# Attention products with v on half-width column tiles, two heads at a time

## Chip, cores and metric

The kernel runs on one core of a Trainium2 chip. The metric is the device time of one execution in microseconds. TensorE is written PE below (PEld for its weight loads), VectorE DVE, ScalarE ACT, GpSimd POOL, SyncE SP.

## What is computed

Causal attention with a learned decay (4 batches, 8 heads, 576 positions, 64 columns a head), then two feed-forward blocks (2304 tokens, 512 -> 2048 -> 512):

```python
cum = np.cumsum(np.log(np.clip(f, 0.0001, 1.0)), axis=-1)
scores = np.matmul(q, k.transpose(0, 1, 3, 2)) / np.sqrt(D) + cum[:, :, :, None] - cum[:, :, None, :]
attn = softmax(np.where(causal, -1e9, scores))
x = np.matmul(attn, v)                        # 2304 x 512
x = (s * np.maximum(x @ w_in, 0) ** 2 + b) @ w_out
x = leaky_relu(x @ w2_in, 0.01) @ w2_out
```

Nearly every operand of a product is kept as a sum of two parts, a rounded one and its rest, so that a product of two such operands is made of three or four products.

## The kernel before

**Units.** Attention is cut into units of one batch: its queries 0 to 255 (`first`) or 256 to 575 (`rest`). Unit 0 has a path of its own (`first_a` to `first_c`). Units 1 to 3 are `first` units, 4 to 7 `rest` units. A unit has 8 heads, taken as 4 pairs. A `first` pair gives two tiles, one per head, each with both query blocks of 128. A `rest` pair gives five: query block 3 for each head, block 2 for each head, and one **half** tile, in which the last 64 queries of both heads stand side by side.

**Stages of a tile.** `st_score` makes the scores on PE (line 296: two heads on different halves of the array's rows), adds the decay and finds the maximum on DVE (line 327), and exponentiates on ACT (line 345). `st_split` divides by the sum and stores p as two float16 parts: line 370 on ACT the rounded one, line 371 on DVE the rest, into `p_hl` (three buffers). A DMA transpose issued from SP then writes `p_t` (three buffers). `st_av` multiplies: for each block of 128 keys and each part of p, line 393 loads as weights both parts of v, 64 columns each, side by side on the array's 128 columns, and streams the transposed p. PSUM tile `ps_v` so holds two halves, p times the rounded v in one half of the partitions and p times the rest in the other. Line 412 copies one half to `x_raw` on ACT, line 413 adds the other on DVE. When both heads of a pair are there, lines 427 and 428 split x into two float32r parts for the first feed-forward block, and for the half tile line 423 scales x on POOL and a DMA stores it for the last unit.

**What sets the order.** `slots_to` issues the stages of tile i, i-1 and i-2 (`LAG` is 2) between the 16 blocks of the first feed-forward layer of an earlier unit (`mlp1_h` line 705, `mlp1_o` lines 746 and 749, with g made in lines 727 to 730). Inside that a list scheduler places each instruction by priority; `run_on` ties the products of one `st_av` call to each other, from the second one on. Each engine then works strictly in the order written. The second layer (lines 807 and 823) comes when all attention is done.

Of the kernel before, what the change touches and what calls it, by code (L numbers as in the profile page):

```python
# [8 lines left out]
F32 = mybir.dt.float32  # L9
F32R = mybir.dt.float32r  # L10
F16 = mybir.dt.float16
# [3 lines left out]
ALU = mybir.AluOpType  # L15
AX = mybir.AxisListType

P = 128
UN = 256
# [19 lines left out]
def attention_moe_moe_kernel(  # L39
# [15 lines left out]
    nc = tc.nc  # L55
    B, H, D, S = vT.shape
# [10 lines left out]
    NL = S - 2 * UN  # L67
# [125 lines left out]

    qk_p, cumk, v_raw, v_st, v_inv = {}, {}, {}, {}, {}
    s_t, t_t, p_hl, p_t, av_t, sm_t = {}, {}, {}, {}, {}, {}
    xs, x_raw = {}, {}

    def load_pair(p):
        if p >= NP:
# [66 lines left out]
    def run_on(first):  # L266
        return nullcontext() if first else tc.high_priority(offset=P_RUN)
# [82 lines left out]
    def last_of_pair(jb):  # L350
        u, h, j, half = jobs[jb]
        return half or (h % 2 == 1 and units[u][2] == UN)

    def st_split(i):

        jb, n, ts, last = tiles[i]
        nt = len(ts)
        tt, sm = t_t.pop(i), sm_t.pop(i)
        nc.vector.tensor_scalar(sm[:, 4 : 4 + nt], sm[:, 2 : 2 + nt], 1.0e-9, 1.0 / PSCALE, ALU.add, ALU.mult)
        nc.vector.reciprocal(sm[:, 6 : 6 + nt], sm[:, 4 : 4 + nt])  # L360
        ph = ap.tile([P, 10 * P], F16, tag="p_hl", name="p_hl", bufs=3)
        at = to = 0
        for r, t in enumerate(ts):
            w = sum(QT[t])
            nk = -(-w // P)
            e, inv = tt[:, at : at + w], sm[:, 6 + r : 7 + r]
            v = ph[:, to : to + 2 * nk * P].rearrange("p (l c) -> p l c", l=2)
            if nk * P > w:
                nc.gpsimd.memset(v[:, :, w:], 0.0)
            nc.scalar.mul(v[:, 0, :w], e, inv)  # L370
            nc.vector.scalar_tensor_tensor(v[:, 1, :w], e, inv, v[:, 0, :w], ALU.mult, ALU.subtract)  # L371
            at += w
            to += 2 * nk * P
        p_t[i] = pt = ap.tile([P, 10, P], F16, tag="p_t", name="p_t", bufs=3)
        nc.sync.dma_start_transpose(out=pt[:, : to // P], in_=ph[:, :to])

    def st_av(i):
        jb, n, ts, last = tiles[i]
        u, h, j, half = jobs[jb]
        b, u0, un, _ = units[u]  # L380
        if half or (n == 0 and h % 2 == 0):
            av_t[j // 2] = ps_a.tile([P, 512], F32, tag="ps_v", name="ps_v", bufs=2)
        av, pt = av_t[j // 2], p_t.pop(i)
        to = 0
        for t in ts:
            q0, m = QT[t]
            nk = -(-(q0 + m) // P)
            at = 0 if half else q0 - u0 + h % 2 * UN
            for e in range(P // m):
                for k in range(nk):  # L390
                    for l in range(2):
                        with run_on(t == ts[0] and e == k == l == 0):
                            nc.tensor.matmul(  # L393
                                av[:, at + e * m : at + (e + 1) * m],
                                v_st[j + e][:, k].rearrange("p l d -> p (l d)"),
                                pt[:, to + l * nk + k, e * m : (e + 1) * m],
                                start=(k == 0 and l == 0),
                                stop=(k == nk - 1 and l == 1),
                            )
            to += 2 * nk  # L400
        if not last:
            return
        pr = h // 2
        if not half and h % 2 == 0:
            x_raw[u] = xp.tile([P, UN + NL], F32, tag="x_raw", name="x_raw", bufs=2)
        xr = x_raw[u]
        at = UN if half else 0
        for e in range(2) if half else [h % 2]:
            own, oth = slice(e * D, (e + 1) * D), slice((1 - e) * D, (2 - e) * D)
            m = NL if half else UN  # L410
            src, o = av[:, e * m : (e + 1) * m], xr[own, at : at + m]
            nc.scalar.copy(o, src[oth])
            nc.vector.tensor_tensor(out=o, in0=src[own], in1=o, op=ALU.add)
        if not last_of_pair(jb):
            return
        if pr == 0:
            xs[u] = xp.tile([P, 2, ND, UN], F32R, tag="x", name="x", bufs=2)
        inv = v_inv[j - j % 2][:, 4:5]
        with ahead(P_X):
            split_x1(xs[u], pr, xr[:, :UN], inv)  # L420
            if un > UN:
                xl = xr[:, UN:]
                nc.gpsimd.tensor_scalar(xl, xl, inv, 0.0, ALU.mult, ALU.add)
                nc.sync.dma_start(out=xld[pr * P : (pr + 1) * P, b * NL : (b + 1) * NL], in_=xl)

    def split_x1(x, d, raw, inv):
        nc.scalar.mul(x[:, 0, d], raw, inv)
        nc.vector.scalar_tensor_tensor(x[:, 1, d], raw, inv, x[:, 0, d].bitcast(F32), ALU.mult, ALU.subtract)
# [151 lines left out]
    def first_b(h):  # L580
# [4 lines left out]
        at = 0  # L585
# [2 lines left out]
            nc.gpsimd.tensor_scalar(e[:, at : at + w], e[:, at : at + w], r[:, t : t + 1], 1.0, ALU.mult, ALU.mult)  # L588
            at += w
        ps = ps_a.tile([P, 512], F32, tag="ps_v", name="ps_t0", bufs=2)  # L590
        pt = pt_0[h] = ap.tile([P, 5 * P], F32, tag="p_t", name="pt_0", bufs=3)

        to = 0
        for k in range(NT0):
# [369 lines left out]
```

## Time and profile before

| | us |
|---|---|
| median of 3 runs | 1044.53 |
| lowest, highest | 1044.37, 1044.60 |
| the profiled execution | 1039.49 |
| its span, first to last instruction | 1037.7 |
| PE busy | 986.1 |
| DVE busy | 537.9 |
| ACT busy | 521.3 |
| products with v (line 393), PE busy | 59.7 |

The profile is that of one execution, which took 5.0 us less than the median. "Busy" counts the time in which an engine has at least one instruction in work; the matmuls of PE overlap, so what one costs is read from start to start on the timeline. The rows on which the prediction rests stand below.

### The profile page before, as it was taken

To read this page: it belongs to the slowest core of one execution; us is meant where nothing else is said; L and a number is where in the kernel's file an instruction comes from. 1 tells how busy PE (TensorE), PEld (TensorE's weight loads), DVE (VectorE), ACT (ScalarE), POOL (GpSimd) and SP (SyncE) were. 2 spreads that over 40 slices of the span, in tenths; PEclk is the share of its full clock that TensorE was granted. 3 is DMA by queue.
4 is the path that set the end of the run, shared out by engine and by line. 5 is a ranking of instruction groups with operands and counts; after the bars stand their busy time and mean duration, and the time that the engine had idled before them with its cause. 6 is when DMAs were issued, how large, how long until landed. Compare 5 with 4: busy or idle time off the path is not lost.

```text
span 1037.7 us, 18127 instructions
## 1 busy us (share of the span) xinstructions
PE 986.1 (95%) x6664; PEld 851.0 (82%) x6664; DVE 537.9 (52%) x1410; ACT 521.3 (50%) x1283; POOL 151.8 (15%) x234
## 2 busy tenths in 40 slices
PE   7887789989999999999999999999999999999998
PEld 4676679879888888888999998778888888888897
DVE  6899773665667766777531399873111311211111
ACT  4777696655656766677643566552221221221232
POOL 4434424110101010100000135430000000000000
PEclk9899999999999999999999999999999999999999
DMA  8499491566889999989620463701000100100010
GB/s 282 152 245 269 89 211 40 136 134 134 186 155 181 180 179 197 185 170 192 90 83 2 168 239 94 239 13 49 33 1 1 61 1 1 41 0 1 1 41 21
DMA packets 184296, 116.68 MB, mean 112 GB/s; under 512 B 137040, under 2 KB 163152, under 8 KB 184208
## 3 DMA queue, kind: packets, MB, share of 16 engines
q1 hardware_dynamic: 184208, 115.53, 47.0%
q8 instruction: 52, 0.85, 0.3%
q14 instruction: 36, 0.29, 0.1%
HBM read 74.00 MB, written 10.04 MB: 81 GB/s over the span
## 4 chain that ended last, share of the span: by engine, by line
PE 47%; issue 3%; DVE 3%; POOL 2%; DMA 1%; ACT 1%; POOLq 0%; SPq 0%; ACTq 0%; DVEq 0%
PE ps_o L823 17%; PE ps_h L807 16%; PE ps_o L749 6%; PE ps_h L705 6%; POOL w L111 2%; PE ps_v L393 1%; DVE wt L103 1%; DMA w_raw<-in_moe_w_out 1%; DVE wt L105 1%; DVE wt L102 1%; PE ps_s L296 1%; DMA p_t<-p_hl 0%; ACT wt L101 0%; PE ps_s L283 0%; DVE g L730 0%
## 5 line engine op out<-in xcount | busy, mean ns | idle before, releaser
L705 PE MATMUL ps_h<-x,w 128*128 128x256 f32 x1728 | 242.9, 286 | 5.0 <-POOL w L111 3.3
L749 PE MATMUL ps_o<-g,w 128*128 128x256 f32 (+1 forms) x1536 | 226.8, 289 | 10.8 <-ACT g L729 6.3
L705 PEld LDWEIGHTS ps_h<-x,w 128*128 128x128 f32 x1728 | 220.4, 190 | 7.7 <-POOL w L111 3.9
L823 PE MATMUL ps_o<-w,g 128*128 128x512 f32 x864 | 216.1, 396 | 1.8 <-DVE g L815 1.8
L807 PE MATMUL ps_h<-x,w 128*128 128x512 f32 (+1 forms) x960 | 213.6, 370 | 0.0
L749 PEld LDWEIGHTS ps_o<-g,w 128*128 128x128 f32 x1536 | 197.3, 190 | 17.5 <-ACT g L729 7.9
L807 PEld LDWEIGHTS ps_h<-x,w 128*128 128x128 f32 x960 | 169.0, 188 | 34.4
L823 PEld LDWEIGHTS ps_o<-w,g 128*128 128x128 f32 x864 | 160.5, 188 | 41.5 <-DVE g L815 3.5
L815 DVE TENSOR_TENSOR g<-ps_h,g 128x512 fp32r<-128x512 f32 (+1 forms) x80 | 51.0, 637 | 258.3 <-ACT g L814 258.1
L813 ACT ACTIVATE ps_h<-ps_h 128x512 f32<-128x512 f32 (+1 forms) x80 | 43.1, 539 | 250.7 <-PE ps_h L807 250.7
L345 ACT ACTIVATE tt<-tt,sm 128x512 f32<-128x512 f32 (+4 forms) x128 | 76.0, 594 | 46.5 <-DVE sm L327 45.2
L371 DVE SCALAR_TENSOR_TENSOR p_hl<-tt,sm,p_hl 128x512 f16<-128x512 f32 (+4 forms) x128 | 77.5, 619 | 34.3 <-ACT p_hl L370 33.8
L370 ACT ACTIVATE p_hl<-tt,sm 128x512 f16<-128x512 f32 (+4 forms) x128 | 73.2, 595 | 40.2 <-DMA p_t<-p_hl 31.6
L111 POOL TENSOR_TENSOR w<-wt,w 128x512 fp32r<-128x512 f32 x48 | 73.6, 1537 | 98.0 <-ACT w L110 92.2
L730 DVE TENSOR_TENSOR g<-ps_h,g 128x256 fp32r<-128x256 f32 x128 | 53.6, 421 | 60.9 <-ACT g L729 59.6
L393 PE MATMUL ps_v<-p_t,v_st 128*128 128x128 f16 (+1 forms) x912 | 59.7, 211 | 14.7 <-DMA p_t<-p_hl 11.9
L727 ACT ACTIVATE ps_h<-ps_h 128x256 f32<-128x256 f32 x128 | 46.8, 367 | 50.3 <-PE ps_h L705 49.4
L393 PEld LDWEIGHTS <-v_st 128*128 128x128 f16 x912 | 44.3, 98 | 21.4 <-issue 13.2
L327 DVE CUSTOM_DVE_ANT_0 tt<-ps_s,cumk 128x512 f32<-128x512 f32 (+4 forms) x128 | 59.6, 497 | 2.2 <-PE ps_s L287 0.7
L101 ACT ACTIVATE wt<-w_raw 128x512 f32<-128x512 f32 x64 | 42.7, 672 | 28.2 <-POOL w L111 19.8
L729 ACT CAST g<-ps_h 128x256 fp32r<-128x256 f32 x128 | 47.2, 370 | 7.9 <-PE ps_o L749 4.4
L728 ACT ACTIVATE ps_h<-ps_h 128x256 f32<-128x256 f32 x128 | 46.9, 368 | 3.0
(91 smaller groups left out, 859.9 us busy)
## 6 DMA issues: line engine op xcount, KB each, us to landing
w_raw<-in_moe_w_in SPq DMA_DIRECT2D x32, 512.0 KB, 5.3
w_raw<-in_moe_w_out SPq DMA_DIRECT2D x32, 512.0 KB, 5.8
cumk<-cumd SPq DMA_DIRECT2D x32, 256.0 KB, 3.9
qk_p<-in_qk SPq DMA_DIRECT2D x16, 480.0 KB, 4.8
x1d<-x1o SPq DMA_DIRECT2D x36, 128.0 KB, 2.9
cumk<-cumd SPq DMA_DIRECT2D x32, 144.0 KB, 3.1
v_raw<-in_v SPq DMA_DIRECT2D x16, 288.0 KB, 3.3
out<-o SPq DMA_DIRECT2D x18, 256.0 KB, 2.3
```

Of the source, the lines that this page charges most:

```text
L111: nc.gpsimd.tensor_tensor(w[:, 1], x, w[:, 0].bitcast(F32), ALU.subtract)
L327: nc.vector.tensor_tensor_reduce(tt[:, at + k0 : at + k0 + kw], ps[:, c, :kw] if half else ps[:, h % 2, at : at + w], cumk[jb][:, k0 : k0 ...
L345: nc.scalar.activation(e, e, AF.Exp, bias=sm[:, r : r + 1], scale=-1.0, accum_out=sm[:, 2 + r : 3 + r])
L370: nc.scalar.mul(v[:, 0, :w], e, inv)
L371: nc.vector.scalar_tensor_tensor(v[:, 1, :w], e, inv, v[:, 0, :w], ALU.mult, ALU.subtract)
L393: nc.tensor.matmul(av[:, at + e * m : at + (e + 1) * m], v_st[j + e][:, k].rearrange("p l d -> p (l d)"), pt[:, to + l * nk + k, e * m : ( ...
L705: nc.tensor.matmul(ps, wi[:, a, d * P : (d + 1) * P], x[:, c, d], start=(d == 0 and n == 0), stop=(d == ND - 1 and n == 2),)
L730: nc.vector.tensor_tensor(out=g[:, 1, :UN], in0=ps, in1=g[:, 0, :UN].bitcast(F32), op=ALU.subtract)
L749: nc.tensor.matmul(po[d], wo[:, a, d * P : (d + 1) * P], g[:, c], start=(first and n == 0), stop=(last and n == 2),)
L807: nc.tensor.matmul(ps[:, :n], wi[:, a, d * P : (d + 1) * P], x[:, e, d, :n], start=(d == 0 and k == 0), stop=(d == ND - 1 and k == 2),)
L815: nc.vector.tensor_tensor(out=g[:, 1, :n], in0=raw, in1=g[:, 0, :n].bitcast(F32), op=ALU.subtract)
L823: nc.tensor.matmul(po[m], g[:, a, m * P : (m + 1) * P], wo[:, e, :], start=(i == 0 and k == 0), stop=(i == NF - 1 and k == 2),)
```

## The change

`st_av` returns at once for the first head of a pair and works at the second head for both. For each block of 128 keys it makes four products per head (each part of v with each part of p), each with 64 columns of weights: head 0 on columns 0 to 63 of the array and partitions 0 to 63 of PSUM, head 1 on columns 64 to 127 and partitions 64 to 127. The four accumulate in PSUM, so that the tile holds x for both heads, and the half tile's queries lie behind the other 256 in the same `ps_v` tile. `x_raw` with its copies and sums is gone, `split_x1` reads PSUM, and the half tile is scaled on ACT. The transposed p has five buffers.

```diff
@@ -193,7 +193,7 @@
 
     qk_p, cumk, v_raw, v_st, v_inv = {}, {}, {}, {}, {}
     s_t, t_t, p_hl, p_t, av_t, sm_t = {}, {}, {}, {}, {}, {}
-    xs, x_raw = {}, {}
+    xs = {}
 
     def load_pair(p):
         if p >= NP:
@@ -371,56 +371,50 @@
             nc.vector.scalar_tensor_tensor(v[:, 1, :w], e, inv, v[:, 0, :w], ALU.mult, ALU.subtract)
             at += w
             to += 2 * nk * P
-        p_t[i] = pt = ap.tile([P, 10, P], F16, tag="p_t", name="p_t", bufs=3)
+        p_t[i] = pt = ap.tile([P, 10, P], F16, tag="p_t", name="p_t", bufs=5)
         nc.sync.dma_start_transpose(out=pt[:, : to // P], in_=ph[:, :to])
 
     def st_av(i):
         jb, n, ts, last = tiles[i]
         u, h, j, half = jobs[jb]
         b, u0, un, _ = units[u]
-        if half or (n == 0 and h % 2 == 0):
-            av_t[j // 2] = ps_a.tile([P, 512], F32, tag="ps_v", name="ps_v", bufs=2)
-        av, pt = av_t[j // 2], p_t.pop(i)
-        to = 0
+        if not half and h % 2 == 0:
+            return
+        j -= j % 2
+        if not half and n == 0:
+            av_t[j] = ps_a.tile([P, 512], F32, tag="ps_v", name="ps_v", bufs=2)
+        av = av_t[j]
+        pts = [p_t.pop(i)] if half else [p_t.pop(i - 1), p_t.pop(i)]
+        to, first = 0, True
         for t in ts:
             q0, m = QT[t]
             nk = -(-(q0 + m) // P)
-            at = 0 if half else q0 - u0 + h % 2 * UN
-            for e in range(P // m):
-                for k in range(nk):
-                    for l in range(2):
-                        with run_on(t == ts[0] and e == k == l == 0):
+            at = q0 - u0
+            for k in range(nk):
+                for lv, lp in ((0, 0), (0, 1), (1, 0), (1, 1)):
+                    for e in range(2):
+                        q = pts[0][:, to + lp * nk + k, e * m : (e + 1) * m] if half else pts[e][:, to + lp * nk + k]
+                        with run_on(first):
                             nc.tensor.matmul(
-                                av[:, at + e * m : at + (e + 1) * m],
-                                v_st[j + e][:, k].rearrange("p l d -> p (l d)"),
-                                pt[:, to + l * nk + k, e * m : (e + 1) * m],
-                                start=(k == 0 and l == 0),
-                                stop=(k == nk - 1 and l == 1),
+                                av[e * D : (e + 1) * D, at : at + m],
+                                v_st[j + e][:, k, lv],
+                                q,
+                                start=(k == lv == lp == 0),
+                                stop=(k == nk - 1 and lv == lp == 1),
                             )
+                        first = False
             to += 2 * nk
-        if not last:
+        if not last_of_pair(jb):
             return
         pr = h // 2
-        if not half and h % 2 == 0:
-            x_raw[u] = xp.tile([P, UN + NL], F32, tag="x_raw", name="x_raw", bufs=2)
-        xr = x_raw[u]
-        at = UN if half else 0
-        for e in range(2) if half else [h % 2]:
-            own, oth = slice(e * D, (e + 1) * D), slice((1 - e) * D, (2 - e) * D)
-            m = NL if half else UN
-            src, o = av[:, e * m : (e + 1) * m], xr[own, at : at + m]
-            nc.scalar.copy(o, src[oth])
-            nc.vector.tensor_tensor(out=o, in0=src[own], in1=o, op=ALU.add)
-        if not last_of_pair(jb):
-            return
         if pr == 0:
             xs[u] = xp.tile([P, 2, ND, UN], F32R, tag="x", name="x", bufs=2)
-        inv = v_inv[j - j % 2][:, 4:5]
+        inv = v_inv[j][:, 4:5]
         with ahead(P_X):
-            split_x1(xs[u], pr, xr[:, :UN], inv)
+            split_x1(xs[u], pr, av[:, :UN], inv)
             if un > UN:
-                xl = xr[:, UN:]
-                nc.gpsimd.tensor_scalar(xl, xl, inv, 0.0, ALU.mult, ALU.add)
+                xl = xp.tile([P, NL], F32, tag="x_l", name="x_l", bufs=2)
+                nc.scalar.mul(xl, av[:, UN:un], inv)
                 nc.sync.dma_start(out=xld[pr * P : (pr + 1) * P, b * NL : (b + 1) * NL], in_=xl)
 
     def split_x1(x, d, raw, inv):
@@ -588,7 +582,7 @@
             nc.gpsimd.tensor_scalar(e[:, at : at + w], e[:, at : at + w], r[:, t : t + 1], 1.0, ALU.mult, ALU.mult)
             at += w
         ps = ps_a.tile([P, 512], F32, tag="ps_v", name="ps_t0", bufs=2)
-        pt = pt_0[h] = ap.tile([P, 5 * P], F32, tag="p_t", name="pt_0", bufs=3)
+        pt = pt_0[h] = ap.tile([P, 5 * P], F32, tag="p_t", name="pt_0", bufs=5)
 
         to = 0
         for k in range(NT0):
```

The built program holds 1824 products on 64 columns in place of 912 on 128. Counted over PE's whole order, the form of the array (128 rows by 128 columns, 64 by 128, 128 by 64) changes 256 times, before 119 times.

PE in a `rest` unit before, where the block of products of the second head begins (v_st_5879 is that head's v, p_t_6103 its transposed p, ps_v_6105 the pair's PSUM tile):

```order
L307 LDWEIGHTS ident_h_74
L307 MATMUL ps_s_6266<-mask_h_75,ident_h_74 128x128
L749 MATMUL ps_o_5437<-g_5744,w_1443 128x256 x6
L393 LDWEIGHTS v_st_5879
L393 MATMUL ps_v_6105<-p_t_6103,v_st_5879 128x128
```

The eight products of one head run between those of the feed-forward layer; the first head's block stands in another place.

PE in a `rest` unit now, the same place (v_st_5716 and v_st_5718 are the pair's two heads):

```order
L743 MATMUL ps_o_4570<-g_5551,w_1902 128x256 x6
L699 MATMUL ps_h_5732<-x_4648,w_161 128x256 x2
L398 LDWEIGHTS v_st_5716
L398 MATMUL ps_v_6000<-p_t_5893,v_st_5716 64x128
L398 LDWEIGHTS v_st_5718
L398 MATMUL ps_v_6000<-p_t_5980,v_st_5718 64x128
```

The two heads alternate, each with its own load, for 32 products; the tile of 256 queries and the half tile follow as runs of 24 and 40.

ACT before, at the end of a `rest` pair (lines 727 to 729 make g, 763 ends a unit):

```order
L412 COPY x_raw<-ps_v 64x256
L728 ACTIVATE ps_h<-ps_h 128x256
L729 CAST g<-ps_h 128x256
L427 ACTIVATE x<-x_raw,vs 128x256
L412 COPY x_raw<-ps_v 64x64
L763 ACTIVATE x1o<-ps_o,sb 128x256
L345 ACTIVATE tt,sm<-tt,sm 128x576
```

ACT now, at the end of such a pair (lines 721 to 723 make g):

```order
L723 CAST g<-ps_h 128x256
L421 ACTIVATE x<-ps_v,vs 128x256
L345 ACTIVATE tt,sm<-tt,sm 128x576
L417 ACTIVATE x_l<-ps_v,vs 128x64
L370 ACTIVATE p_hl<-tt,sm 128x576
```

The copies are gone, and a scaling of 64 columns has come, behind the split.

## Rows read from the trace of the kernel before

**Rows 1.** The page, span and busy time of each engine.

```profile
span 1037.7 us, 18127 instructions
...
PE 986.1 (95%) x6664; PEld 851.0 (82%) x6664; DVE 537.9 (52%) x1410; ACT 521.3 (50%) x1283; POOL 151.8 (15%) x234
```

**Rows 2.** Stretches: length, busy PE, PEld, DVE, ACT, POOL (instructions), clock, DMA share, GB/s.

```profile
40.00:160.00 120.00, 100.38 (x720) 88.09 (x719) 102.40 (x326) 90.21 (x261) 44.34 (x37) 0.95 0.77 188
160.00:520.00 360.00, 345.28 (x3110) 307.97 (x3109) 236.44 (x735) 237.95 (x613) 39.94 (x97) 1.00 0.79 155
520.00:600.00 80.00, 80.00 (x672) 79.90 (x672) 26.89 (x61) 36.79 (x97) 6.02 (x35) 1.00 0.27 94
```

**Rows 3.** Groups by shape: products with v, what reads them, their split.

```profile
L393 PE MATMUL ps_v<-p_t,v_st 128*128 128x128 f16 x592 | 47.8, 221 | 14.1 <-DMA p_t<-p_hl 11.2 <-DMA v_st<-v_hl 2.8
...
L413 DVE TENSOR_TENSOR x_raw<-ps_v,x_raw 64x256 f32<-64x256 f32 x56 | 23.5, 419 | 7.9 <-ACT x_raw L412 7.0
...
L412 ACT COPY x_raw<-ps_v 64x256 f32<-64x256 f32 x56 | 20.6, 367 | 1.7 <-PE ps_v L393 0.3
...
L427 ACT ACTIVATE x<-x_raw,vs 128x256 fp32r<-128x256 f32 x28 | 14.0, 502 | 6.1 <-DVE x_raw L413 4.3 <-PE ps_h L705 1.5
...
L393 PE MATMUL ps_v<-p_t,v_st 128*128 128x64 f16 x320 | 12.1, 193 | 0.6 <-DMA p_t<-p_hl 0.6
...
L763 ACT ACTIVATE x1o<-ps_o,sb 128x256 f32<-128x256 f32 x18 | 8.5, 472 | 11.8 <-DMA x1d<-x1o 9.2 <-PE ps_o L749 1.8 <-DVE bw L761 0.7
...
L412 ACT COPY x_raw<-ps_v 64x64 f32<-64x64 f32 x32 | 6.6, 207 | 1.8 <-PE ps_v L393 1.1
```

**Rows 4.** Timeline of PE, 250 to 262 us (start, us, line, xcount).

```profile
254.19 1.57 PE L705 MATMUL ps_h<-x,w 128*128 128x256 f32 x12
255.59 1.57 PE L749 MATMUL ps_o<-g,w 128*128 128x256 f32 x12
...
258.43 0.51 PE L393 MATMUL ps_v<-p_t,v_st 128*128 128x128 f16 x6
258.77 1.19 PE L283 MATMUL ps_s<-qk_p 128*128 128x288 f32 x4
...
259.83 0.75 PE L393 MATMUL ps_v<-p_t,v_st 128*128 128x64 f16 x20
260.41 1.68 PE L749 MATMUL ps_o<-g,w 128*128 128x256 f32 x12
```

**Rows 5.** Timeline of PE near 251.5 us and, in narrow windows, near 75.5 us.

```profile
251.16 0.63 PE L705 MATMUL ps_h<-x,w 128*128 128x256 f32 x4
251.72 0.92 PE L296 MATMUL ps_s<-qk_p 64*128 64x384 f32 x4
...
75.25 0.92 PE L296 MATMUL ps_s<-qk_p 64*128 64x256 f32 x8
76.10 0.40 PE L307 MATMUL ps_s<-mask_h,ident_h 128*128 128x128 bf16 x4
...
75.57 0.38 PE L296 MATMUL ps_s<-qk_p 64*128 64x256 f32 x2
...
75.78 0.39 PE L296 MATMUL ps_s<-qk_p 64*128 64x128 f32 x4
```

**Rows 6.** Timeline of weight loads, two narrow windows at 251.7 and 251.9 us.

```profile
251.72 0.19 PEld L296 LDWEIGHTS ps_s<-qk_p 64*128 64x128 f32 x2
...
251.83 0.19 PEld L296 LDWEIGHTS ps_s<-qk_p 64*128 64x128 f32 x2
```

**Rows 7.** Who waited for whom, PE (total us, times, longest).

```profile
PE ps_v L393 <- DMA p_t<-p_hl: 11.9, 11, 3.1
PE ps_o L749 <- ACT g L729: 6.3, 6, 1.5
...
PE ps_o L749 <- DVE g L730: 2.8, 9, 0.6
```

**Rows 8.** The page, groups, idle time before ScalarE line 370.

```profile
L370 ACT ACTIVATE p_hl<-tt,sm 128x512 f16<-128x512 f32 (+4 forms) x128 | 73.2, 595 | 40.2 <-DMA p_t<-p_hl 31.6
```

## Prediction

> **What bounds the kernel now.** I read the page first: TensorE is busy for 986.1 of 1037.7 us [rows 1], so an instruction added there costs its time unless it falls into one of the gaps. The table by stretch then says where the gaps are [rows 2]. From 520 to 600 us, when attention is over, there are none. From 160 to 520 us TensorE is busy 345.3 of 360, so 14.7 us are free. From 40 to 160 us it is busy 100.4 of 120, so 19.6 us are free, and VectorE with 102.4 of 120 is the fuller neighbour. All products with v lie between 40 and 520 us. What they do to TensorE's time there moves all that follows, one for one.
>
> Next I read the pace on the timeline. A float32 product of 256 columns takes 1.40/12 = 0.117 us from start to start, one product with v of 128 columns 0.34/6 = 0.057, and one of 64 columns 0.58/20 = 0.029 [rows 4]. So the 912 products cost 592 x 0.057 + 320 x 0.029 = 43 us [rows 3, 4]. The 2-byte weight load is hidden even at 0.029.
>
> The trace has no product that uses half of the array's columns. Its nearest relation is line 296, which uses half of the **rows**: two heads side by side. Their loads start in twos, 0.11 us apart [rows 6], and the products run in twos as well: two pairs of 256 columns and two of 128 fill 75.25 to 76.10 us [rows 5]. The second pair takes 75.78 - 75.57 = 0.21 us, no more than 256 columns for one head alone would. The first takes 0.32, and the two of 128 columns take 0.32 up to line 307 where half of 0.21 each, 0.21, would do. So in this form two heads cost the time of one, but coming into it costs 0.11 us (a load that nothing covers) and leaving it 0.11 (the array runs empty). Ahead of it there is a third piece: four products of line 705 take 0.56 us up to line 296 [rows 5], not 4 x 0.117 = 0.47, so 0.09.
>
> **The sum.** (a) *The products.* For each pair of heads the 912 become 1824 on 64 columns each, that is 592 pairs of 128 columns and 320 pairs of 64. If a pair runs side by side as in rows 5, one of 128 columns takes 0.057 us, as one product did before: 0. For one of 64 columns the two loads set the pace. The trace bounds the load of 64 columns by 0.029 us, what the 2-byte load of 128 columns fits into [rows 4], and by 0.11, the float32 load of 128 columns [rows 6]. I take half of the latter, 0.053, since loads on half of the array come at the float32 pace in the only rows there are, and the columns are halved. That is 320 x (0.053 - 0.029) = +7.7 us; the ends are 0 and 320 x 0.08 = 26.
>
> The Trainium skill bears on this choice: "TensorEngine Tiling (Array Packing)", Gotcha 2, says that column tiling excludes fast weight load. By it the term is the +7.7, without it 0; no run here shows a 2-byte load on half of the columns yet.
>
> (b) *The change of form.* TensorE's order holds 70 runs of the new products, 21 for units 1 to 3 and 49 for units 4 to 7; ten blocks have their first product set ahead alone. Each run is a visit to another form: 0.09 to empty the array, 0.05 for the first load (half of 0.11), 0.11 on leaving, and 0.10 for the float32 load behind it that nothing covers, 0.35 us in all. Ends: 0.20 if no load shows, 0.41 if each costs 0.11. For the 49: +17.2 us. For the 21: +7.3, of which I leave half, 3.7, since 19.6 us of gaps lie there in which TensorE waits for others [rows 2]; ends 0 and 7.3.
>
> (c) *What goes from ScalarE and VectorE.* 56 copies of 367 ns and 32 of 207 leave ScalarE, 27 us, and 16 scalings of 64 columns come from GpSimd, at most 16 x 207 = 3.3 us; 56 sums of 419 ns and 32 shorter ones leave VectorE, over 23.5 us [rows 3]. The split reads PSUM in place of SBUF: line 763, a ScalarE scaling of that shape from PSUM, takes 472 ns [rows 3], so I price that at nothing. Neither engine sets the time after 160 us: they are busy 238 and 236 of 360 [rows 2]. What can come back is TensorE's waits. It waited 6.3 us for g from ScalarE, 2.8 for g from VectorE and 11.9 in 11 waits for a transposed p [rows 7], 21.0 together. ScalarE stood 31.6 us ahead of line 370 for a transfer to free p_hl [rows 8], with the MLP's three g passes queued behind. Five buffers for the transposed p let that transfer leave earlier. Against that, the first product of a block now needs two transposes, and all of TensorE's queue stands behind that wait. I credit half, -10.5 us; ends 0 and -21.0.
>
> (d) *DMA.* SP issues the same 104 transposes of p and the same 16 stores of the tail. A store now waits on ScalarE instead of GpSimd, with transposes queued behind it. The nearest row is ScalarE's copy of that size, which found its data late by 1.8 us in 32 times [rows 3]; that bounds it at 1 us for 16. I take 0: it delays a transfer, and the waits for those are in (c).
>
> Sum: 7.7 + 17.2 + 3.7 - 10.5 = **+18.1 us**. The profiled execution took 1039.49 us, 1.8 around its span; the median of the runs is 5.0 us above it. I add the sum to the median: 1044.5 + 18 = **1062.5**. This case runs from 1046 (the tail's loads free, the 21 runs free, three quarters of the waits back: 17.2 - 15.7) to 1081 (7.7 + 49 x 0.41 + 21 x 0.41, nothing back).
>
> **Rivals.**
> *One after the other.* If two products on different columns do not overlap, or their loads share one path, each pair of 128 columns costs 0.057 more, 592 x 0.057 = 33.7, and each of 64 columns a second load, 320 x 0.053 = 17.0: +50.7 on top, 1113. For it: no row shows columns shared. Against it: row pairs load and run together [rows 5, 6].
>
> *Loads uncovered.* If a load on these columns waited for the product that runs, a pair would cost 0.057 + 0.053, so 592 x 0.053 + 320 x 0.029 = +40.7 on top, 1103. Against it: in rows 6 the second pair of loads starts 0.11 us behind the first, while the products of 251.72 run on the same rows. The Trainium skill has this as a rule ("TensorE: Matmul & The Clock Gate", Part 3): a load overlaps running products only when its row group differs, and here all use all rows. Rows 6 speak against it.
>
> *Waits were the price (faster).* Place: the 15 us of gaps from 160 to 520 us. If a change of form costs only the 0.09 and no load shows, the 70 runs cost 6 us, the tail's loads keep 0.029, and all 21.0 us of waits go: -15, 1030. It decides where a run costs less than 21/70 = 0.30 us; rows 5 say 0.35.
>
> *No difference.* The credits equal the visits: 1044.
>
> **Chances.** Side by side as summed 0.64, one after the other 0.14, loads uncovered 0.08, faster 0.10, no difference 0.04. The prediction is the first case. A measurement of this kernel tells 0.2%, 2 us, from no change, so slower is 0.64 + 0.14 + 0.08 = 0.86, same 0.04, faster 0.10. The range goes from the lower end of the first case, 1046, to 1116, which takes in both slower rivals' middles; it leaves out 0.14 below and some 0.05 above.
>
> **What would show it.** Products with v in twos a few ns apart, pairs every 0.057 us and in the tail every 0.053; loads of 64 columns longer than the 2-byte loads of 128; a gap of 0.2 us on entering a run and about 0.2 on leaving, with "issue" as its cause; 160 to 520 us longer by 14 to 25 us, after it the same. Starts 0.057 apart for each single product would mean the first rival, 0.11 per pair the second. A run that enters and leaves without a gap, and p waits gone, would prove the forecast wrong on the other side.

## The result and the profile after

The changed kernel took 1050.95 us (median of 13 runs, 1048.18 to 1054.84) against 1044.60 (1041.19 to 1047.91) for the kernel before in the same measurement: a ratio of 1.0067 [1.0054, 1.0080], 6.4 us slower. The forecast was 18 us slower, so the direction held and the size did not. 1050.95 lies inside the stated range of 1046 to 1116, near its lower end.

The profiled execution of the change took 1052.05 us, 1.1 above its median; that of the kernel before lay 5 us below its median. The two profiles therefore differ by 12.6 us where the medians differ by 6.4, and a difference between single profiles is trusted below only where runs confirm it.

The page of the change, to be read beside [rows 1, 8]:

```profile
span 1050.2 us, 19781 instructions
...
PE 1004.4 (96%) x7576; PEld 862.4 (82%) x7576; DVE 516.4 (49%) x1322; ACT 492.8 (47%) x1211; POOL 140.7 (13%) x218
...
L370 ACT ACTIVATE p_hl<-tt,sm 128x512 f16<-128x512 f32 (+4 forms) x128 | 71.9, 596 | 39.4 <-DMA p_t<-p_hl 18.1
```

Its stretches, beside [rows 2], and its groups by shape, beside [rows 3]:

```profile
40.00:160.00 120.00, 105.12 (x789) 90.83 (x788) 103.66 (x321) 85.52 (x251) 40.18 (x38) 0.91 0.78 193
160.00:520.00 360.00, 351.13 (x3848) 308.16 (x3847) 209.85 (x649) 210.87 (x543) 35.01 (x81) 0.99 0.79 154
```

```profile
L398 PEld LDWEIGHTS <-v_st 128*64 128x64 f16 x1824 | 46.9, 111 | 15.1 <-issue 4.9 <-DMA v_st<-v_hl 2.5
L398 PE MATMUL ps_v<-p_t,v_st 128*64 128x128 f16 x1184 | 43.7, 221 | 4.5 <-DMA p_t<-p_hl 2.5 <-DMA v_st<-v_hl 1.9
...
L398 PE MATMUL ps_v<-p_t,v_st 128*64 128x64 f16 x640 | 13.2, 197 | 0.0
L421 ACT ACTIVATE x<-ps_v,vs 128x256 fp32r<-128x256 f32 x28 | 13.0, 465 | 6.7 <-PE ps_h L699 3.5 <-PE ps_v L398 3.2
```

ScalarE and VectorE lost the work that the diff takes from them (521.3 to 492.8 and 537.9 to 516.4 us busy), and the split that now reads PSUM takes 465 ns in place of 502 [rows 3]. TensorE's idle time from 40 to 520 us fell from 34.3 us [rows 2] to 14.9 + 8.9 = 23.8.

The timeline of PE in the change, around one run of products at 253 us and one of the tail at 261 us, read in narrow windows (start, us, line, tile, xcount):

```profile
252.88 0.22 PE L307 MATMUL ps_s<-mask_h,ident_h 128*128 128x128 bf16 x1
253.03 0.86 PE L398 MATMUL ps_v<-p_t,v_st 128*64 128x128 f16 x24
...
253.56 0.33 PE L398 MATMUL ps_v<-p_t,v_st 128*64 128x128 f16 x6
...
253.61 0.28 PE L398 MATMUL ps_v<-p_t,v_st 128*64 128x128 f16 x4
253.82 0.39 PE L743 MATMUL ps_o<-g,w 128*128 128x256 f32 x1
...
254.05 0.40 PE L743 MATMUL ps_o<-g,w 128*128 128x256 f32 x2
...
260.76 0.82 PE L398 MATMUL ps_v<-p_t,v_st 128*64 128x64 f16 x40
...
261.32 0.26 PE L398 MATMUL ps_v<-p_t,v_st 128*64 128x64 f16 x6
```

Of the 24 products the first starts at 253.03, the last six at 253.56 and the last four at 253.61. So ten pairs take 0.58 us, 0.058 a pair with the uncovered first load in it, which leaves the 0.056 to 0.057 that one product took before [rows 4]. Two heads cost the time of one. In the tail the first 34 of 40 products, 17 pairs, take 261.32 - 260.76 = 0.56 us, 0.033 a pair, again with the first load in it.

Around the run the form is paid for. From line 307 to the first product it is 253.03 - 252.88 = 0.15 us, 0.09 more than the pace. The last two pairs and the way out take 253.82 - 253.61 = 0.21, 0.10 more than 2 x 0.056. The first float32 product behind it takes 254.05 - 253.82 = 0.23, 0.11 more than the pace of 0.117 [rows 4]. With 0.02 for the first load, a visit costs 0.31 to 0.32 us.

Not all of that is new. In [rows 4] the kernel before takes 1.68 us for twelve products of line 749 behind its products with v (from 260.41), and 1.57 for twelve behind other float32 products (from 255.59): it pays the same 0.11 for the float32 load, and its order holds 96 separate runs of products with v, that of the change 70. New in a visit are 0.09 + 0.02 + 0.10 = 0.21 us.

Who waited for whom on PE in the change, beside [rows 7] (total us, times, longest):

```profile
PE ps_o L817 <- ACT g L808: 6.9, 1, 6.9
...
PE ps_o L743 <- DVE g L724: 3.8, 7, 1.3
...
PE ps_v L398 <- DMA p_t<-p_hl: 2.5, 2, 1.9
...
PE ps_o L743 <- ACT g L723: 1.9, 3, 0.9
```

The three waits that the forecast spoke of fell from 21.0 to 8.2 us. A new one of 6.9 us stands at the head of the table, and it lies outside attention, where the second feed-forward layer begins (line 801 makes h there, 807 applies the leaky ReLU, 808 stores the rounded g, 817 multiplies it; the kernel before has them at 807, 813, 814 and 823). This beginning, the joint, on PE, first in the kernel before and then in the change:

```profile
625.44 2.90 PE L807 MATMUL ps_h<-x,w 128*128 128x512 f32 x12
...
635.84 0.86 PE L823 MATMUL ps_o<-w,g 128*128 128x512 f32 x3
```

```profile
632.08 2.92 PE L801 MATMUL ps_h<-x,w 128*128 128x512 f32 x12
...
653.43 2.92 PE L817 MATMUL ps_o<-w,g 128*128 128x512 f32 x6 [6.92 <-ACT g L808]
```

When this layer begins, the profile of the change is 6.6 us behind. At the end of the span it is 12.5 behind, so 5.9 arise in this layer. From its first product to the end of the span it takes 412.1 to 412.3 us in each of the twelve profiles that leave its work as it is and have no such wait, and 418.1 here. ScalarE at the joint, in the change (timeline):

```profile
643.73 0.59 ACT L807 ACTIVATE ps_h<-ps_h 128x512 f32<-128x512 f32 x1
...
646.79 0.57 ACT L807 ACTIVATE ps_h<-ps_h 128x512 f32<-128x512 f32 x1
...
650.06 0.58 ACT L807 ACTIVATE ps_h<-ps_h 128x512 f32<-128x512 f32 x1
...
652.80 1.56 ACT L808 CAST g<-ps_h 128x512 fp32r<-128x512 f32 x3
```

Three passes of line 807 stand ahead of the first line 808, with weight conversions (lines 101 and 110) between them. The cause is a place in SBUF, read from the built programs. `x_raw` had two buffers of 320 float32 columns, `x_l` has two of 64, so the pool is 2048 bytes a partition smaller and the pool behind it, with `x1o`, moves by as much: from bytes 208352 to 210400 to bytes 210400 to 212448. The first g of the second layer lies at 210912 to 215008, now across `x1o`. So the first line 808 has to wait for the stores of `x1o` to HBM (in the program it waits for three DMA queues; in the kernel before for ScalarE alone), and the scheduler sets it back in ScalarE's order.

### The profile page after: what moved, and what is told of

Its sections match the earlier page's. It is cut to its first block, busy times and chain, and to the rows that moved or that the text cites. A ratio compares the mean times of both kernels' runs of the same rounds, so it can differ in the third digit from the quotient of the medians.

```text
span 1050.2 us, 19781 instructions
## 1 busy us (share of the span) xinstructions
PE 1004.4 (96%) x7576; PEld 862.4 (82%) x7576; DVE 516.4 (49%) x1322; ACT 492.8 (47%) x1211; POOL 140.7 (13%) x218
## 4 chain that ended last, share of the span: by engine, by line
PE 53%; DVE 3%; DMA 3%; issue 1%; POOL 1%; ACT 1%; SPq 0%; POOLq 0%; ACTq 0%; DVEq 0%
PE ps_o L817 19%; PE ps_h L801 18%; PE ps_o L743 7%; PE ps_h L699 6%; PE ps_v L398 1%; DMA w_raw<-in_moe_w_out 1%; POOL w L111 1%; PE ps_s L296 1%; DMA x1d<-x1o 1%; DVE wt L103 0%; DMA p_t<-p_hl 0%; DVE wt L105 0%; DVE g L724 0%; PE ps_s L283 0%; DMA v_st<-v_hl 0%
## 5 line engine op out<-in xcount | busy, mean ns | idle before, releaser
L743 PE MATMUL ps_o<-g,w 128*128 128x256 f32 (+1 forms) x1536 | 223.0, 289 | 14.4 <-DVE g L724 3.8
L743 PEld LDWEIGHTS ps_o<-g,w 128*128 128x128 f32 x1536 | 196.1, 190 | 23.8 <-DVE g L724 7.3
L801 PEld LDWEIGHTS ps_h<-x,w 128*128 128x128 f32 x960 | 169.0, 188 | 34.3
L371 DVE SCALAR_TENSOR_TENSOR p_hl<-tt,sm,p_hl 128x512 f16<-128x512 f32 (+4 forms) x128 | 80.9, 655 | 22.5 <-ACT p_hl L370 21.4
L370 ACT ACTIVATE p_hl<-tt,sm 128x512 f16<-128x512 f32 (+4 forms) x128 | 71.9, 596 | 39.4 <-DMA p_t<-p_hl 18.1
L111 POOL TENSOR_TENSOR w<-wt,w 128x512 fp32r<-128x512 f32 x48 | 68.9, 1437 | 103.0 <-ACT w L110 97.0
L721 ACT ACTIVATE ps_h<-ps_h 128x256 f32<-128x256 f32 x128 | 47.0, 368 | 73.2 <-PE ps_h L699 73.2
L398 PE MATMUL ps_v<-p_t,v_st 128*64 128x128 f16 (+1 forms) x1824 | 56.9, 213 | 4.5 <-DMA p_t<-p_hl 2.5
L398 PEld LDWEIGHTS <-v_st 128*64 128x64 f16 x1824 | 46.9, 111 | 15.1 <-issue 4.9
L103 DVE SCALAR_TENSOR_TENSOR wt<-w_raw,wt 128x512 int32<-128x512 int32 x64 | 50.3, 790 | 1.0
```

Of the source, the lines that this page charges most:

```text
L111: nc.gpsimd.tensor_tensor(w[:, 1], x, w[:, 0].bitcast(F32), ALU.subtract)
L398: nc.tensor.matmul(av[e * D : (e + 1) * D, at : at + m], v_st[j + e][:, k, lv], q, start=(k == lv == lp == 0), stop=(k == nk - 1 and lv == ...
L743: nc.tensor.matmul(po[d], wo[:, a, d * P : (d + 1) * P], g[:, c], start=(first and n == 0), stop=(last and n == 2),)
L801: nc.tensor.matmul(ps[:, :n], wi[:, a, d * P : (d + 1) * P], x[:, e, d, :n], start=(d == 0 and k == 0), stop=(d == ND - 1 and k == 2),)
```

## The experiments

**The joint, and the number of buffers.** The first kernel is the change with `x_l` padded to the size of `x_raw` (the padded kernel below); it needs the room of one p buffer, so it has four. The second has the four buffers alone.

```diff
-                xl = xp.tile([P, NL], F32, tag="x_l", name="x_l", bufs=2)
+                xl = xp.tile([P, UN + NL], F32, tag="x_l", name="x_l", bufs=2)[:, :NL]
...
-        p_t[i] = pt = ap.tile([P, 10, P], F16, tag="p_t", name="p_t", bufs=5)
+        p_t[i] = pt = ap.tile([P, 10, P], F16, tag="p_t", name="p_t", bufs=4)
```

> The change with the scratch tile of the half tile made as large as x_raw was, so that the second layer's first g lies in SBUF where it lay before, and with four buffers for the transposed p, since five do not fit beside it. Theory 'joint': some 6 of the change's 6.3 us come from the second layer's first g, which the new layout puts onto x1o and so behind its stores. It expects a time within 2 us of before, ratio 0.998 to 1.002, and no wait of 6.9 us of TensorE on ScalarE line 808. Theory 'form' (the changes of array form are the whole cost): as the change, ratio 1.005 to 1.008.

Measured: 1045.65 us, ratio 1.0010 [0.9994, 1.0027].

> The change with four buffers for the transposed p in place of five, layout at the joint left as the change has it; TensorE's order is that of the run above. Theory 'joint': the fifth buffer does nothing, ratio 1.005 to 1.008, as the change, and the 6.9 us wait stays. Theory 'buffers' (the fifth buffer gave waits back): slower than the change by 3 us or more, ratio over 1.009.

Measured: 1050.95 us, 1.0060 [1.0038, 1.0082]. The first lines of PE's waits, of this kernel:

```profile
PE ps_v L398 <- DMA p_t<-p_hl: 7.2, 6, 2.5
PE ps_o L817 <- ACT g L808: 7.0, 1, 7.0
```

The padded kernel has no such wait. Its ScalarE at the joint:

```profile
641.87 0.58 ACT L807 ACTIVATE ps_h<-ps_h 128x512 f32<-128x512 f32 x1
642.49 0.59 ACT L808 CAST g<-ps_h 128x512 fp32r<-128x512 f32 x1
```

TensorE's order is the same in both for the first 5543 of 7336 products, all of attention among them, and parts at the joint. So the place of the tile alone is worth 1050.95 - 1045.65 = 5.3 us: nearly the whole of the measured loss. The second layer takes 412.2 us in the profile of the padded kernel and 417.8 in the other. The fifth buffer shows no gain (1050.95 with five and with four, in orders that part at the 782nd product). Without the joint the change, with four buffers, is level with the kernel before, with three.

In one and the same order of attention the wait for p reads 7.2 us above and here, in the padded kernel,

```profile
PE ps_v L398 <- DMA p_t<-p_hl: 3.9, 4, 2.0
```

so a difference of 3 us between the waits of two profiles shows nothing.

**Fewer visits.** Block 2 and the half tile were put into one run, and the second head ahead of the first in each two, on the padded kernel: 45 runs in place of 72, and 206 changes of form in TensorE's order where the padded kernel has 260 and the kernel before 119.

```diff
         if not half and h % 2 == 0:
             return
+        if last and not last_of_pair(jb):
+            return
+        if half:
+            av_run(i - 1, True)
+            av_run(i, False)
+        else:
+            av_run(i, True)
...
-                    for e in range(2):
+                    for e in (1, 0):
```

> As the first of these runs, but the second block of a pair is multiplied together with the half tile in one run, and the second head comes first in each two, so that no first product stands alone: 45 runs on half columns instead of 72, changes of form 206 instead of 260. Theory 'form' (each run costs 0.31 us that is paid): 27 x 0.31 = 8 us less than the first run, ratio about 0.992. Rival 'gaps' (runs fall into time in which TensorE would wait anyway): within 2 us of the first run.

Measured: 1056.44 us, 1.0101 [1.0077, 1.0125]: slower by 11 us than the padded kernel, with a third fewer runs. PE's waits in it:

```profile
PE ps_v L409 <- DMA p_t<-p_hl: 10.0, 6, 2.9
PE ps_o L754 <- DVE g L735: 6.0, 9, 2.0
...
PE ps_o L754 <- ACT g L734: 4.0, 4, 2.3
```

They sum to 20.0 us, nearly the 21.0 of before the change; the wait for p alone is 10.0 against 3.9 in the padded kernel. That fits a simple reading: each run now waits for more transposes at a time. It is not the only one, since the granted clock fell too (mean of the runs 0.982, 0.988 in the padded kernel). Shown is that a third fewer visits did not make the kernel faster.

The half of that edit that only turns the heads round, on the padded kernel:

> The change in its old layout and with four buffers, with the second head first in each two products, so that no block's first product stands alone ahead of the rest: 60 runs instead of 72, 237 changes of form instead of 260, nothing merged and no transposed p held longer. Theory 'form': 12 x 0.31 = 3.7 us less than without, ratio about 0.997, most of it before 190 us. Rival: the early runs lie in time in which TensorE waits anyway, ratio 1.000 to 1.002.

Measured: 1039.51 us, 0.9954 [0.9937, 0.9971], 5.8 us less than the padded kernel. It saves 23 changes of form, under 12 visits, so 3.7 us at most; the rest comes from something else, and the order differs from the 176th product on. The kernel with merged runs, which has this order of heads too, stands 1.0101 - 0.9954 = 0.0147, 15 us, above it.

**More visits.** One full-width product with zero weights was put between the first and second key block of each block of queries: 60 more times out of the form and back.

```diff
+                if k == 0 and nk > 1:
+                    with run_on(False):
+                        nc.tensor.matmul(av[:, at : at + NL], zero_h, ident_h[:, :NL], start=False, stop=False)
```

> The change in its old layout and with four buffers, with one product of zero weights on all 128 columns put into each of the 60 blocks of products, after its first block of keys: it adds nothing to the result and changes the form twice more, 377 changes for 260. From rows of the change's trace such a visit costs 0.09 + 0.09 to empty the array, 0.02 for the load and 0.03 for the product, about 0.24 us. Theory 'form': 60 x 0.24 = 14 us more than the run without them, ratio about 1.014. Rival 'gaps': under 5 us more, ratio under 1.006.

Measured: 1047.84 us, 1.0039 [1.0025, 1.0053]: 0.0029, about 3 us, over the padded kernel, where 60 x 0.24 = 14 us would be paid if nothing hid them. The stretch from 160 to 520 us in the padded kernel:

```profile
160.00:520.00 360.00, 347.77 (x3804) 303.95 (x3805) 211.53 (x652) 213.49 (x544) 34.24 (x80) 0.99 0.79 154
```

and with the visits doubled:

```profile
160.00:520.00 360.00, 354.17 (x3838) 306.32 (x3837) 210.37 (x646) 212.47 (x542) 34.01 (x79) 1.00 0.79 154
```

The added visits went into idle time: 12.2 us of it became 5.8. (A change of form counts as busy here: its 0.1 us lies under the modelled ends of the products ahead of it. Idle time is steadier than the waits: the unpadded kernel with four buffers has 11.7 in this stretch.) Of PE's wait for p this is left:

```profile
PE ps_v L400 <- DMA p_t<-p_hl: 1.5, 3, 0.7
```

One thing may flatter the result. The granted clock was higher with the doubled visits, 0.991 against 0.988 in the mean of twelve runs each. An estimate: 0.0034 of 1046 us is 7 us less at half the clock, where a product takes 0.43 us in place of 0.233 (the joint, last section), and so 3 us. So the added visits cost 3 us, or 6 at most, of 14.

**Is a visit cheap, or is it hidden?** In attention every edit also changes the scheduler's order. In the second layer TensorE is busy for all 300.00 us from 700 to 1000. There 80 pairs of products with zero weights were added to the kernel before with four buffers: on half the columns each in the first kernel, on all columns in the second. Both have the same order of products.

```diff
+                if m == 0 and k == 1:
+                    for r in (slice(0, D), slice(D, P)):
+                        nc.tensor.matmul(po[m][r, :NL], zero_h[:, r], ident_h[:, :NL], start=False, stop=False)
```

> The kernel before with four buffers (1037.3 when it ran) and, in the second layer, where TensorE works without a wait, 80 visits to the column form: after the second of the three products that add g times the output weights to a block, two products with zero weights of 64 columns each (columns 0 to 63, then 64 to 127) on 64 moving columns are added. Theory, a visit costs what the trace of the change shows (0.09 us to enter, 0.08 us for the pair, 0.09 us to leave, 0.11 us of uncovered load of the next 4-byte weights, less what a product in the ordinary form costs): 80 x 0.30 to 0.37 = 24 to 30 us more than without. Rival, a visit is cheap by itself: under 10 us more.

> The same with two products with zero weights of 128 columns on 64 moving columns at the same 80 places, so that the form never changes. Theory: each pair costs the loads and products themselves and the next 4-byte load: 80 x 0.1 to 0.2 = 8 to 16 us more than without, and 10 to 20 us less than the run with the change of form. Rival: within 4 us of it, so that the change of form has no price of its own.

Measured: 1063.50 us, 1.0200 [1.0160, 1.0239], and 1047.85 us, 1.0053 [1.0027, 1.0079]. In the profiles the layer takes 438.9 and 423.7 us, and 412.2 without the pairs: 26.6 and 11.4 us for 80, 0.33 and 0.14 us each, their two products with them. The PE timeline of one visit, in narrow windows (line 825 is the layer's product, 0.233 us from one to the next):

```profile
799.58 0.40 PE L825 MATMUL ps_o<-w,g 128*128 128x512 f32 x1
799.91 0.22 PE L831 MATMUL ps_o<-ident_h,zero_h 128*64 128x64 bf16 x2
800.06 0.50 PE L825 MATMUL ps_o<-w,g 128*128 128x512 f32 x1
...
800.39 0.39 PE L825 MATMUL ps_o<-w,g 128*128 128x512 f32 x1
```

and the same place without a change of form:

```profile
800.21 0.40 PE L825 MATMUL ps_o<-w,g 128*128 128x512 f32 x1
800.45 0.23 PE L831 MATMUL ps_o<-ident_h,zero_h 128*128 128x64 bf16 x2
800.51 0.48 PE L825 MATMUL ps_o<-w,g 128*128 128x512 f32 x1
...
800.83 0.39 PE L825 MATMUL ps_o<-w,g 128*128 128x512 f32 x1
```

Into the form 0.33 against 0.24 us, through and out of it 0.15 against 0.06; the load behind is uncovered in both (0.33 and 0.32). The change of form there and back costs 15.65/80 = 0.20 us, and the whole visit its full 0.33, where TensorE has no wait to put it in; 0.14 of that is paid without any change of form. So a visit is not cheap; in attention most of it is hidden.

The Trainium skill says in "TensorEngine Tiling (Array Packing)", Key Properties, that changing the tiling mode drains TensorE, without a figure. The trace agrees: 0.09 us each way.

**What was thought to be relief.** First the kernel before with four p buffers and nothing else:

```diff
-        p_t[i] = pt = ap.tile([P, 10, P], F16, tag="p_t", name="p_t", bufs=3)
+        p_t[i] = pt = ap.tile([P, 10, P], F16, tag="p_t", name="p_t", bufs=4)
```

> The kernel before with four buffers for the transposed p instead of three. Theory 'waits': TensorE's 11.9 us of waits for the transposed p hang on that third buffer; some 4 us or more less, ratio under 0.996. Rival: those waits are the transfer's own time behind the split; within 2 us of before.

Measured: 1037.31 us (1034.08 to 1039.60, 6 runs), 0.9918 [0.9896, 0.9940], the fastest of all and faster than both kernels. PE's longest waits in it fell only a little:

```profile
PE ps_v L393 <- DMA p_t<-p_hl: 9.2, 7, 2.4
PE ps_o L749 <- ACT g L729: 5.3, 7, 1.8
```

Then the same without the copies and sums:

```diff
-            nc.scalar.copy(o, src[oth])
-            nc.vector.tensor_tensor(out=o, in0=src[own], in1=o, op=ALU.add)
...
-            split_x1(xs[u], pr, xr[:, :UN], inv)
...
+            if not half:
+                split_x1(xs[u], pr, av[:, :UN], inv)
...
```

> The kernel before with four buffers, without the copy and the sum that join the two parts of each head (left out: that sum, so x is made of one head's two parts); the split reads PSUM and the half tile is scaled on ScalarE, as in the change. It takes 27 us off ScalarE and 30 us off VectorE and leaves TensorE's form alone. Theory 'relief' (that work held g back): 3 us or more under before with four buffers, ratio under 0.989. Rival: those engines have room, and it is within 2 us of it, 0.990 to 0.994.

Measured: 1040.68 us, 0.9971 [0.9955, 0.9987]. Some 50 us of work of two engines gone, and 0.0053, 5.5 us, slower than with it: no relief shows. The order differs from the 182nd product on, and the split no longer comes behind the half tile, so a relief smaller than what an order moves could lie hidden in it.

Then four buffers with both heads' products issued together at full width:

```diff
     def st_av(i):
+        if tiles[i][0] < len(jobs) and not jobs[tiles[i][0]][3]:
+            if jobs[tiles[i][0]][1] % 2 == 0:
+                return
+            av_one(i - 1)
+        av_one(i)
...
```

> The kernel before with four buffers for the transposed p, and the products of a pair's two heads issued together once the second head is reached, each on the full 128 columns as before, with the copy and the sum as before. What is left between it and the change in its old layout (1.001 against before) is the column form and the evacuation. Theory 'form': the 8 us between those two are what the column form costs net, and grouping the heads costs nothing: ratio 0.990 to 0.994, as before with four buffers. Theory 'grouping': waiting for both heads is what costs: ratio 0.998 to 1.003.

Measured: 1046.21 us, 1.0019 [1.0002, 1.0035], 10 us over the same with the heads apart, without any column form. And with the second head's products first:

```diff
-            av_one(i - 1)
+            av_one(i)
+            av_one(i - 1)
+            return
         av_one(i)
...
```

> The kernel before with four buffers and the products of both heads issued together, at full width, as in the run that took 1046.2, but with the second head's products ahead of the first's, so that all wait for the later transposition. If the second head first gained 5.8 us in the column form because it saved changes of form (23 of them), nothing is gained here: 1045 to 1048. If it gained because a lone first product no longer waits at the head of TensorE's order, 1040 to 1042.

Measured: 1043.95 us, 0.9995 [0.9973, 1.0018], between the two expectations, so it does not tell them apart.

These two are also the column form's nearest partners, with both heads together and four buffers. In the first order of the heads, full width measures 1.0019 and columns 1.0010 (the padded kernel); with the second head first, 0.9995 and 0.9954. In neither is the column form dearer, though it has 72 and 60 visits and the other none. At full width, in the first order, PE waits far longer:

```profile
PE ps_v L400 <- DMA p_t<-p_hl: 15.8, 9, 4.4
PE ps_o L756 <- ACT g L736: 6.7, 5, 2.9
...
PE ps_o L756 <- DVE g L737: 2.6, 7, 1.0
```

That is 25.1 us, against 3.9 + 2.5 + 4.7 = 11.1 in the padded kernel, as it would be if visits stood where waits were. It is no clean price of the form, because the copies and the granted clock differ too (0.981 against 0.988). What both pay is the wait for both heads, 10 us over the heads apart with four buffers; the forecast had named it in (c), without a price. The column form with three buffers was not run, so how much of the fourth buffer's gain lies in the 1.0010 stays open.

**Do the transfers set the pace?** The transfers of the second head's decay sums were left out (28 of the 88 transfers, 5632 of 15872 KB; those of the half tiles stay), in the kernel before, with four buffers, and in the changed one with the second head first:

```diff
+        if not half and h % 2 == 1:
+            cumk[jb] = cumk[jb - 1]
+            return
```

> The kernel before, in which the second head of each two works on the decay sums of the first head (its own are not loaded, so the decay of every second head is left out): half of these transfers go, nothing else. If the transfers set the pace of the attention stretch (DMA share 0.84 to 0.93 between 280 and 520 us), it gains 10 us or more. If the pace is that of TensorE and of the chain score, exp, split, transposition, it stays within 3 us of 1044.5.

> The same edit on the kernel before with four buffers for the transposed p (1037.3 when it ran, by 0.992 of the kernel before). If the four buffers gained by letting the transfers run on, less is left for this edit than in the kernel before with three buffers. If transfers are not the bound, it stays at 1034 to 1040.

> The same edit on the change with the large x_l tile, four buffers and the second head first (1039.5 when it ran). Theory: in the column form TensorE's own time, changes of form among it, fills the stretch, so fewer transfers give no more than 3 us: 1036 to 1041. Rival: the products of both heads wait in common for late transfers, so this form gains more from the edit than the form before does: 1030 or less.

Measured: 1046.60 us, 1.0027 [1.0008, 1.0045]; 1043.80, 1.0007 [0.9985, 1.0029]; 1039.05, 0.9949 [0.9930, 0.9968]. In the first the DMA share of the full part of attention came down from

```profile
280.00:400.00 120.00, 114.79 (x1054) 100.56 (x1052) 83.55 (x263) 80.61 (x210) 10.78 (x33) 1.00 0.93 178
400.00:520.00 120.00, 117.60 (x1097) 104.46 (x1097) 82.80 (x257) 83.47 (x215) 9.28 (x27) 1.00 0.86 164
```

in the kernel before to

```profile
280.00:400.00 120.00, 115.43 (x1052) 101.51 (x1051) 85.95 (x269) 81.36 (x211) 12.16 (x33) 1.00 0.81 163
400.00:520.00 120.00, 116.16 (x1081) 102.72 (x1081) 83.69 (x262) 82.75 (x214) 9.76 (x28) 1.00 0.79 155
```

and nothing was gained in any of the three. That speaks against transfers as the bound, though the share fell by a tenth only and the order moved too. The second result is a warning. With four buffers, less to load made the kernel 0.0089, 9 us, slower. TensorE's order differs between the two from the 173rd product on. Four buffers in place of three gained 0.0082, 8.6 us, with all transfers and 0.0020, 2 us, with fewer (with intervals that overlap). The order differs between three and four buffers as well, from the 805th product on, so the gain may belong to an order as much as to a buffer.

Of the kernels without the stall at the joint, the three column kernels that keep the runs apart and add nothing lie at 0.9949, 0.9954 and 1.0010 (236 to 260 changes of form), those at full width between 0.9918 and 1.0027 (119 to 121). The two sets overlap. One order in both forms was not tried, so the price of the form inside attention can't be read closer than that.

## Why the prediction was wrong in size

**(a) The products: 7.7 us forecast, 1.3 at most measured.** The step that failed is the load of 64 columns. It was priced at 0.053 us by the float32 loads on half of the rows [rows 6]; tail pairs run at 0.033 us at most, where one product took 0.029, and full ones at 0.056, so the loads are hidden. The lower end, 0, was nearly the value. The rival that loads are uncovered fell with it. The kernel before with four buffers shows the 2-byte load at full width:

```profile
L393 PEld LDWEIGHTS <-v_st 128*128 128x128 f16 x912 | 44.2, 98 | 17.8 <-issue 11.2 <-DMA v_st<-v_hl 2.7
```

A load of half as many columns takes 111 ns in the change where this one takes 98, so the Trainium skill's rule that column tiling has no fast weight load ("TensorEngine Tiling (Array Packing)", Gotcha 2) fits the load itself; the time that was drawn from it did not come. The Trainium skill's rule beside the rival, as it is worded, did not hold here ("TensorE: Matmul & The Clock Gate", Part 3): loads on the other columns did run under products on all rows.

**(b) The change of form: 20.9 us forecast as paid.** The size of a visit was right: 0.35 us forecast, 0.31 to 0.32 measured in attention, 0.33 in the second layer. Two steps failed. The first is "0.10 for the float32 load behind it that nothing covers". The kernel before pays that load too [rows 4], behind 96 runs where the change has 70, so it is no part of a difference: 0.10 for the 49 and half of the 21 is 6.0 of the 20.9. The second is "For the 49: +17.2", that is, charging them whole. The stretch had 14.7 us of gaps [rows 2], and a visit fills a gap as a product does: 60 more visits cost 3 us of 14, 6 at most. The reason for which half was left off the first 21, gaps in the same stretch, held for the 49 as well.

**(c) The relief: -10.5 us forecast.** The waits named fell by 12.8 us between the two profiles, near the forecast, and ScalarE's wait ahead of line 370 from 31.6 to 18.1 [rows 8], as it said. But neither the work taken from ScalarE and VectorE (1040.68 without the copies against 1037.31 with them) nor the fifth buffer shows as time. The reading that fits the runs is that TensorE came later to its waits, because the visits stood there: idle time is 12.2 us with the visits and 5.8 with them doubled. By it the rest of (b) and (c) were one term, counted once as a price and once as a relief. That reading is supported and not shown, since every run of it has an order of its own.

**(d) DMA: 0 forecast.** Leaving out a third of what the decay sums move gained nothing in three kernels, so the delay of a few others is not likely to show.

**Missed: +5.3 us behind attention.** "After it the same" was wrong. The diff shrinks a tile in a pool that another stage's tile lies behind, and the price stands in a stage that the diff does not touch.

In all: attention was forecast at 18.1 us and is worth 1 (1.0010 [0.9994, 1.0027], in the padded kernel with four buffers), so -0.6 to 2.8. Of the 17 too many, 6.4 to 7.7 are the tail's loads, 6.0 the load that was paid before too, and the rest, 3 to 5, fits visits that stand in waits. With 5.3 for the joint the sum is 6.3, against 6.4 measured; that close an agreement is luck, as the intervals and the different order of five buffers allow some 2 us either way. Of the rivals, products one after the other fell with the pairs. The rival of waits as the price named the right place, the gaps, and failed at its price of a visit (0.09; 0.21 is new) and at the joint. "No difference" describes attention, and not the kernel.

Left open: why one order of the same products is up to 10 us faster than another. The runs show that an order can move the time by more than the form does; they don't show which wait in it does.

## What to carry to other kernels

An instruction added to an engine that is 96% busy costs its time only where that engine doesn't wait: look for the idle time of the same stretch first, charge only what the kernel before does not pay already, and don't book the filled waits a second time as relief from something else. A tile that grows or shrinks moves those behind it; compare where later stages' tiles lie and what their first writes wait for, as the 5.3 us here came from that alone. Where a scheduler makes the order, a gain or loss of 1% from an edit in it may belong to the order, and a size varied by one (buffers, the order of two heads) belongs in the same measurement.

## What the runs showed of the hardware

Two products on different halves of the columns start 3 to 4 ns apart and run side by side, a pair of 128 moving columns every 0.056 us, although each product has its own load of 64 columns, 111 ns long. Entering and leaving the form costs 0.09 us each way, and the float32 load behind it is uncovered, 0.09 to 0.11 us, with or without a change of form. The stall at the joint also cost clock, in the change:

```profile
646.50:653.40 6.90, 0.01 (x1) 0.00 (x0) 6.54 (x9) 4.32 (x9) 3.14 (x3) 0.85 0.95 287
651.40:658.20 6.80, 4.77 (x11) 3.80 (x12) 6.54 (x9) 4.51 (x8) 3.31 (x3) 0.50 0.98 352
```

TensorE waited from 646.5 to 653.4 us. Its granted clock fell during that wait and stood at 0.50, 1.2 GHz, from 651.4 to 658.2, until 4.8 us after TensorE had begun again. The eleven products of that time come 4.77/11 = 0.43 us apart, where 0.233 is the pace at 2.4 GHz: 2.2 us lost. With the wait that is 9.1, and the layer is 5.9 longer; the kernel before has pauses around four waits of line 823 between 651 and 695 us that the change has not, which make up the rest.
